# Two transformer layers on one core: the next block's preparation cut into single-engine steps, its stores on one queue, and a new timetable

## The chip, the cores and the metric

The kernel runs on one core of a Trainium2 chip. The metric is device time in microseconds (us) of the whole program, from the runs listed below. The engines are named as the profile names them: PE (TensorE, the matmuls), PEld (its weight loads), DVE (VectorE), ACT (ScalarE), POOL (GpSimd) and SP (SyncE, which here only issues DMA transfers). An engine carries out its instructions in program order. A letter q behind an engine's name (SPq, ACTq) marks an instruction that its sequencer issues, such as a DMA.

## The reference

Two layers, each an attention block and a gated block over 2048 tokens of width 448 (16 heads of 28, inner width 1792):

```python
x = A_x
for layer in range(2):
    # attention
    q, k, v = split_heads(layernorm(x) @ A_wqkv)
    x = x + merge_heads(softmax(q @ k.T * 28 ** -0.5) @ v) @ A_wo
    # gated
    n = layernorm(x)
    x = x + (sigmoid(n @ B_w_gate) * (n @ B_w_up)) @ B_w_down
```

Both layers use the same weights. All tensors are float32; the kernel computes the products from float16 high and low parts.

## The kernel before, in words

**Blocks and pairs.** In the gated part (`gated`, from L1342) the 2048 tokens are four blocks of 512, and the 1792 inner columns are seven pairs of 256. The work is done pair by pair: block 0 pairs 0 to 6, then block 1, and so on. For one pair `gate_and_up` (from L1503) multiplies the block's normalized tokens with the gate weights (m = 0) and the up weights (m = 1) by a seven-product scheme on half matrices. Its PE order is: `first(0)`, `first(1)`, `apart(0)`, `second(0)`, `second(1)`, `apart(1)`, `third(0)`, `third(1)`, `c11_c22(0)`, `c11_c22(1)`, `c21(0)`, `c21(1)`, `c12(0)`, `c12(1)`. After `first`, `second` and `third` ACT copies a PSUM bank called chain to the tiles one and two (L1509). After `c11_c22` DVE adds the bank side to one (L1525, called "the adds" below, one for each m); `c12` writes the same side bank, so PE cannot start `c12(0)` before the first add is done. Then ACT takes the sigmoid and DVE multiplies.

**Places.** Between these products there are six places, `along(0)` to `along(5)`, where other work is put: place 0 after `first(1)`, 1 after `second(1)`, 2 after `third(1)`, 3 after `c11_c22(1)`, 4 after the multiplications that follow `c21`, 5 at the pair's end. In place 0 and 1 go the splits of the pair before (`parts`, `rest`, L1393) and the addition of a finished part of the output to x. From block 1 on, PE also gets there the down products of the block before (`pieces`, bank dnp, L1436). Block 1 has four of these in a pair, since block 0's first three pairs use another path (`down`, L1484 to L1486); blocks 2 and 3 have seven.

**Preparation of the next block.** While block b is multiplied, block b + 1 is prepared by a list of steps, taken from a queue (`run_fill`); `portions(b, p)` says how many are taken in which place of which pair. For a block of the gated part the list was 16 steps: four of `norm` (row statistics, on DVE, with two small POOL operations each), four of `squares` (DVE scales a 128-token tile into xn, L288, and transposes it in 32 by 32 squares into xs, L305), one `store` and `gather` (four DMAs write xs to memory, L317; two read it back as xraw, transposed, L325 and L327), and seven of `half_steps`. These form differences t1 to t4 of quarters of xraw on DVE (`subtract`), and split seven operands into a float16 high part (ACT) and a low part (DVE: value minus high part) in xwide and xshort (`divide`); for the last three ACT copies half of the high part's tail (`double`, L389). The last block of layer 0 prepares the next layer's first two blocks with the same `store` and another ending; the last block of layer 1 prepares nothing.

**Slots and weights.** SBUF tiles of one size come from 19 slots in a first-in, first-out list of free ones (`Slots`): a tile that is given back goes to the end of the list, and the next tile to be made takes the one at its head. Whoever writes the new tile waits for the readers of the old one. xn, xs, xraw, xwide and xshort take slots of the same list as the weights. When a pair is done, its two weight slots are given back and the two weight loads (gu, m = 0 and m = 1) for the pair after the next are put on POOL's queue (`used_gu`, L1327), and from block 1 on one down weight (dn, L1339) behind them. POOL issues in order, so a load that waits for its slot holds those behind it.

Of the kernel before, what the change touches and what calls it, by code (L numbers as in the profile page):

```python
# [110 lines left out]
def interleaved_layers(ctx: ExitStack, tc: tile.TileContext, x_in, wqkv, wo, w_gate, w_up,  # L111
                       w_down, out):
    nc = tc.nc
# [7 lines left out]
    qrt = Slots(spool, "q", N_QUART)  # L121
# [133 lines left out]
    class Block:  # L255
# [86 lines left out]

        def steps(self):
            return self.squared() + [
                lambda: (self.store((nc.sync, nc.scalar)), self.gather())] + (
                        self.half_steps() if self.halves else
                        [lambda: self.ready(0, 1), lambda: self.ready(2, 3)])

# [4 lines left out]
        def half_steps(self):  # L353
            def cut(k, t):

                if self.turned:
                    return self.raw[:, k:k + 2, t * P:(t + 2) * P]
                return self.raw[:, k:k + 2, :].rearrange(
                    "p k (i t c) -> p k t i c", i=4, t=TB)[:, :, t:t + 2]

            def ordered(v):
                return v.rearrange("p k (t i c) -> p k t i c", t=2, i=4)

            def subtract(name, a, b):
                t = qrt.get(name, [P, 2, W // 2])
                if self.turned:
                    nc.vector.tensor_tensor(t, a, b, op=ALU.subtract)
                    return t
                a, b = [v if len(v.shape) == 5 else ordered(v) for v in (a, b)]
                for k in range(2):  # L370
                    nc.vector.tensor_tensor(ordered(t)[:, k], a[:, k], b[:, k],
                                            op=ALU.subtract)
                return t

            def divide(to, v):

                hi, lo = to[:, 0], to[:, 1]
                if len(v.shape) == 5:
                    for k in range(2):
                        nc.scalar.copy(ordered(hi)[:, k], v[:, k])  # L380
                        nc.vector.tensor_tensor(ordered(lo)[:, k], v[:, k], ordered(hi)[:, k],
                                                op=ALU.subtract)
                else:
                    nc.scalar.copy(hi, v)
                    nc.vector.tensor_tensor(lo, v, hi, op=ALU.subtract)

            def double(to):

                nc.scalar.copy(to[64:P, 0, 1], to[0:64, 0, 1])  # L389

            def r11():
                self.wide = big.get("xwide", [P, 4, 2, 2, W // 2], F16)
                self.short = big.get("xshort", [P, 3, 2, 2, W // 2], F16)
                self.t1 = subtract("t1", cut(0, 2), cut(0, 0))
                divide(self.wide[:, 0], cut(0, 0))

            def t1():
                self.t2 = subtract("t2", cut(2, 2), self.t1)
                divide(self.wide[:, 1], self.t1)
                qrt.put(self.t1)  # L400

            def t2():
                self.t3 = subtract("t3", cut(2, 2), cut(0, 2))
                divide(self.wide[:, 2], self.t2)

            def t3():
                self.t4 = subtract("t4", cut(2, 0), self.t2)
                nc.gpsimd.memset(self.t4[64:P, 1, :], 0.0)
                divide(self.wide[:, 3], self.t3)
                qrt.put(self.t2, self.t3)  # L410

            def r21():
                divide(self.short[:, 0], cut(2, 0))
                double(self.short[:, 0])

            def t4():
                divide(self.short[:, 1], self.t4)
                double(self.short[:, 1])
                qrt.put(self.t4)

            def r22():
                divide(self.short[:, 2], cut(2, 2))
                double(self.short[:, 2])
                big.put(self.raw)

            return [r11, t1, t2, t3, r21, t4, r22]

        def ready(self, *kts):
            if kts[0] == 0:
# [224 lines left out]
    def run_fill(fill, n=1):  # L654
        for _ in range(n):
            if fill:
                fill.popleft()()
# [610 lines left out]
    def out_project(outs, gate):  # L1268
        new_banks()
        nc.scalar.activation(warm, warm, AF.Sigmoid)  # L1270
        nc.scalar.reg_load(gate_scale, back.bitcast(I32)[0:1, 3:4])
        first = Block(0, True)
        steps = deque([first.turn_raw] + first.half_steps())
        early = 6

        def products(pm, t, kts):
            by_tokens(pm, outs.hi(t), outs.lo(t), outs.tail(t) if 3 in kts else None, gate.out,
                      kts)

        def add(pm, t):  # L1280
            nc.vector.scalar_tensor_tensor(x[:, t, :], pm, back[:, 1:2], x[:, t, :],
                                           op0=ALU.mult, op1=ALU.add)

        gate.load_gu()
        gate.load_usual()
        pms = [bank(t, "op")[:, 0:D] for t in range(early)]
        for t in range(early):
            products(pms[t], t, range(3))
        first.begin()
        for t in range(early):  # L1290
            products(pms[t], t, [3])
            add(pms[t], t)
            if t < TB:
                first.stats(t)
            if t >= TB:
                first.scale(t - TB)
        for j in range(early - TB, TB):
            first.scale(j)
        for t in range(early, NT):
            pm = bank(t if t < 8 else t % 4, "op")[:, 0:D]  # L1300
            products(pm, t, range(4))
            add(pm, t)
            if t >= 9:
                run_fill(steps, 2 if t == 9 else 1)
        big.put(*outs.kt, gate.out)
        run_fill(steps, 9)
        return first

# [42 lines left out]
    def gated(layer, first, wt, before_next):  # L1351
# [6 lines left out]
        steps = deque()  # L1358
# [135 lines left out]
        def gate_and_up(blk, w, at, operands):  # L1494
# [46 lines left out]
            def along(i):  # L1541
                for do in at[i]:
                    do()
# [27 lines left out]
            c12(1)  # L1571
            times(two[0][:, lo], two[1][:, lo])
            qrt.put(one[1], two[1])
            along(5)
            if made:
                made.late()
                return made
            hls = []
            for h in (one[0], two[0]):
# [95 lines left out]
    def portions(b, p):  # L1675

        if b == 0:
            steps = {0: {1: 4, 5: 1}, 1: {1: 4}, 2: {2: 1, 5: 2}, 3: {1: 1, 2: 2, 5: 1}}
        elif b < NB - 1:
            steps = {0: {1: 1, 2: 1}, 1: {1: 2, 2: 1}, 2: {1: 1, 2: 1}, 3: {1: 2},  # L1680
                     4: {2: 1, 5: 1}, 5: {1: 1, 2: 1}, 6: {1: 1, 2: 2}}
        else:
            steps = {0: {1: 2, 2: 1}, 1: {1: 2, 2: 1}, 2: {1: 1, 2: 2}, 3: {1: 2, 2: 2},
                     4: {1: 1, 2: 1}, 5: {1: 1, 2: 1}, 6: {1: 1, 2: 2, 5: 1}}
        return [steps.get(p, {}).get(i, 0) for i in range(6)]
# [88 lines left out]
```

## Time and profile before

| | |
|---|---|
| three runs | 1929.95 us median (1929.7 to 1930.24) |
| the profiled execution | 1928.17 us, its span 1926.5 us |
| PE busy | 1897.7 us, 99% of the span |
| DVE, ACT, POOL busy | 1413.9, 1365.6, 240.4 us |
| gated part, layer 0 | about 605 to 967 us of the span |
| gated part, layer 1 | about 1555 us to the end |

The times in the profile's rows count from the span's first instruction. A timeline row gives start, duration, engine, line, operation, the tiles written and read, their sizes and how many instructions were merged; in square brackets it gives how long the engine stood idle before it and what ended the wait. In a row of waits the numbers are the total, the count and the longest.

### The profile page before, as it was taken

How to read it: one execution, taken by the hardware profiler on the slowest of the kernel's cores; microseconds unless marked ns; L12 is line 12 of the kernel's file. 1: busy time of each engine (PE TensorE's matmuls, PEld its weight loads, DVE VectorE, ACT ScalarE, POOL GpSimd, SP SyncE). 2: the span in 40 equal slices, each digit the busy share in tenths (PEclk: the TensorE clock that was granted, in tenths of full speed). 3: DMA queues.
4: the chain of work that ended last, by engine and by line, in shares of the span. 5: the costliest groups of instructions: out<-in, count | busy, mean ns of one | idle time of the engine just before them, and what ended most of it. 6: DMA issues, size and time to landing. Idle time of an engine off the chain costs nothing. (4 is left out here: it accounts for less than half of the span.)

```text
span 1926.5 us, 56325 instructions
## 1 busy us (share of the span) xinstructions
PE 1897.7 (99%) x24317; PEld 1412.7 (73%) x24317; DVE 1413.9 (73%) x2816; ACT 1365.6 (71%) x1742; POOL 240.4 (12%) x467
## 2 busy tenths in 40 slices
PE   9999999999999999999999999999999999999999
PEld 4455655555556798999954578888888667989998
DVE  7648798688877597788664487778777767887764
ACT  5569999999983455454344799999999545554541
POOL 2013312232002021122100000000000011211110
PEclk9999999999999999999999999999999999999999
DMA  5565555354314556657634322112211235676752
GB/s 173 169 201 166 161 145 156 111 157 133 92 65 131 207 203 228 208 216 250 231 94 132 88 50 51 30 48 51 51 29 64 74 124 187 207 276 199 267 203 90
DMA packets 107298, 275.20 MB, mean 143 GB/s; under 512 B 12766, under 2 KB 63086, under 8 KB 106912
## 3 DMA queue, kind: packets, MB, share of 16 engines
q0 software_dynamic: 33088, 165.74, 24.4%
q1 hardware_dynamic: 67120, 102.33, 18.8%
q10 hardware_dynamic: 6832, 3.44, 0.8%
q8 instruction: 192, 3.15, 0.7%
q14 instruction: 66, 0.54, 0.1%
HBM read 213.39 MB, written 50.73 MB: 137 GB/s over the span
## 5 line engine op out<-in xcount | busy, mean ns | idle before, releaser
L1126 ACT ACTIVATE prob_s<-sc 128x1536 f32<-128x1536 f32 x659 | 892.3, 1484 | 6.6 <-PE sc L1111 3.3
L1162 PE MATMUL acc<-prob_s,val_s 128*32 128x256 f32 (+3 forms) x7754 | 595.9, 383 | 0.0
L1111 PE MATMUL sc<-qp_s 114*32 114x512 f16 x7896 | 581.2, 379 | 0.0
L527 PEld LDWEIGHTS <-gu_s 128*128 128x128 f16 x4368 | 427.1, 98 | 71.1 <-issue 23.8
L1111 PEld LDWEIGHTS <-qp_s 114*32 114x32 f16 x8192 | 311.3, 95 | 175.4 <-issue 77.3
L1162 PEld LDWEIGHTS acc<-prob_s,val_s 128*32 128x32 f32 x7754 | 326.2, 110 | 92.3 <-issue 7.3
L527 PE MATMUL chain<-xwide_s,gu_s 128*128 128x256 f16 x2016 | 248.3, 273 | 1.4 <-ACT two_q L1509 0.7
L1436 PE MATMUL dnp<-dn_s,hparts_s 128*128 128x224 f16 x2100 | 236.4, 260 | 0.0
L1436 PEld LDWEIGHTS <-hparts_s 128*128 128x128 f16 x2100 | 202.5, 98 | 5.1
L1509 ACT COPY one_q<-chain 128x256 f32<-128x256 f32 x224 | 81.2, 372 | 139.6 <-PE chain L527 118.0
L1142 DVE SCALAR_TENSOR_TENSOR power_q<-power_q,expo_q 128x512 f32<-128x512 f32 x222 | 153.7, 692 | 7.6
L527 PE MATMUL side<-xshort_s,gu_s 128*128 128x256 f16 x1120 | 141.2, 272 | 14.9 <-DVE one_q L1525 14.8
L512 PE MATMUL qkp<-xhl_s,wqk_s 128*128 128x512 f16 x616 | 138.0, 379 | 0.7 <-DVE xhl_s L491 0.3
L1525 DVE TENSOR_TENSOR one_q<-side,one_q 128x512 f32<-128x512 f32 x112 | 72.0, 685 | 65.0 <-PE side L527 50.5
L512 PEld LDWEIGHTS <-wqk_s 128*128 128x128 f16 x616 | 60.0, 98 | 70.1 <-ACT wqk_s L223 1.0
L1191 DVE STREAM_TRANSPOSE oturned_q<-acc 128x512 f32<-128x512 f32 x32 | 22.9, 716 | 118.4 <-PE acc L1162 118.4
L1327 POOL DMA_DIRECT2D gu_s<-gu_parts x104 | 56.0, 539 | 379.0 <-PE side L527 216.1
L1389 ACT CAST hparts_s<-hsums_q 128x256 f16<-128x256 f32 (+1 forms) x144 | 68.4, 489 | 33.5 <-DVE hsums_q L1401 20.4
L527 PE MATMUL side<-xwide_s,gu_s 128*128 128x256 f16 x672 | 91.7, 273 | 0.0
L1162 PE MATMUL acc<-power_q,val_s 128*32 128x256 f32 (+3 forms) x278 | 86.3, 393 | 0.0
L704 ACT ACTIVATE qkhl_q<-qkp 128x512 f16<-128x512 f32 x56 | 33.2, 593 | 74.0 <-PE qkp L512 70.6
L1536 ACT ACTIVATE one_q<-one_q 128x512 f32<-128x512 f32 x56 | 35.3, 630 | 68.7 <-DVE one_q L1525 68.7
(209 smaller groups left out, 2291.4 us busy)
## 6 DMA issues: line engine op xcount, KB each, us to landing
gu_s<-gu_parts POOLq DMA_DIRECT2D x104, 800.0 KB, 6.0
dn_s<-dn_parts POOLq DMA_DIRECT2D x50, 784.0 KB, 7.1
qp_s<-qk_scr SPq DMA_DIRECT2D x96, 224.0 KB
qk_scr<-qkhl_q SPq DMA_DIRECT2D x56, 256.0 KB
gu_parts<-pack_s POOLq DMA_DIRECT2D x14, 800.0 KB, 4.0
xraw_s<-xt_scr SPq DMA_DIRECT2D x12, 768.0 KB
xt_scr<-xs_s SPq DMA_DIRECT2D x34, 224.0 KB
qp_s<-qk_scr SPq DMA_DIRECT2D x64, 112.0 KB
```

Of the source, the lines that this page charges most:

```text
L512: nc.tensor.matmul(pm, w, x, start=(i == 0), stop=(i == len(terms) - 1))
L527: nc.tensor.matmul(pm, a, x, start=(first and i == 0), stop=(i == len(terms) - 1), skip_group_check=True)
L1111: nc.tensor.matmul(ps[32 * j:32 * j + 32, :], hd.k[:, keys], hd.q[:, qb * W:(qb + 1) * W], start=True, stop=True, tile_position=(0, 32 * j))
L1126: nc.scalar.activation(prob[:, 0:n, :], ps[:, 0:n, :], AF.Exp, scale=exp_scale)
L1142: nc.vector.scalar_tensor_tensor(p, p, c[k], y, op0=ALU.add, op1=ALU.mult)
L1162: nc.tensor.matmul(acc[qb * VC:(qb + 1) * VC, s], v[:, kc % TB, h, :], probs[c * NB + qb][:, s], start=(kc == 0 and a == 0), stop=(kc == N ...
L1327: queue.dma_start(self.gu[-1][m], gu_parts[p, m])
L1389: nc.scalar.copy(to[:, :, 0], a)
L1436: nc.tensor.matmul(pm, a[:, x, t], w[:, p, y], start=(begin and n == 0 and (j == 0 or alone)), stop=(n == 2), skip_group_check=True)
L1509: nc.scalar.copy(to, pm)
L1525: nc.vector.tensor_tensor(one[m], side[m], one[m], op=ALU.add)
L1536: nc.scalar.activation(out, v, AF.Sigmoid, scale=gate_scale)
```

## The change

It has five parts.

1. `divide` becomes `high` (ACT) and `low` (DVE). The high part of an operand is made in one step and its low part in the next one, so that within a step DVE uses nothing that ACT makes in it and ACT nothing that DVE makes in it. `double` is one step later still. The half steps become nine: the last low part and the last `double` are steps of their own (`last_low`, `last_rows`). All instructions are the same as before; only their order is new.
2. `store()` in `steps` is called without queues: all four DMAs go on SP's queue. Before, SP and ACT issued two each.
3. `made.late()` (two DVE subtractions of the pair itself) comes before `along(5)`, not after it.
4. In `portions` the 18 steps are laid out anew for block 0 and for blocks 1 and 2. The last block's row stays.
5. The steps after the attention's output product (`out_project`), which run the same half steps for block 0 itself, are taken 3, 2, 1, 1, ... at a time in place of 2, 1, 1, 1, ...

```diff
         def steps(self):
             return self.squared() + [
-                lambda: (self.store((nc.sync, nc.scalar)), self.gather())] + (
+                lambda: (self.store(), self.gather())] + (
...
             def r11():
...
                 self.t1 = subtract("t1", cut(0, 2), cut(0, 0))
-                divide(self.wide[:, 0], cut(0, 0))
+                high(self.wide[:, 0], cut(0, 0))
 
             def t1():
+                low(self.wide[:, 0], cut(0, 0))
                 self.t2 = subtract("t2", cut(2, 2), self.t1)
-                divide(self.wide[:, 1], self.t1)
+                high(self.wide[:, 1], self.t1)
+
+            def t2():
+                low(self.wide[:, 1], self.t1)
+                self.t3 = subtract("t3", cut(2, 2), cut(0, 2))
+                high(self.wide[:, 2], self.t2)
                 qrt.put(self.t1)
...
-            return [r11, t1, t2, t3, r21, t4, r22]
+            return [r11, t1, t2, t3, r21, t4, r22, last_low, last_rows]
...
             if t >= 9:
-                run_fill(steps, 2 if t == 9 else 1)
+                run_fill(steps, {9: 3, 10: 2}.get(t, 1))
...
             qrt.put(one[1], two[1])
+            if made:
+                made.late()
             along(5)
             if made:
-                made.late()
                 return made
...
         if b == 0:
-            steps = {0: {1: 4, 5: 1}, 1: {1: 4}, 2: {2: 1, 5: 2}, 3: {1: 1, 2: 2, 5: 1}}
+            steps = {0: {1: 4, 5: 5}, 2: {1: 1, 2: 1, 3: 1, 5: 1}, 3: {1: 1, 2: 1, 3: 1, 5: 1},
+                     4: {1: 1}}
         elif b < NB - 1:
-            steps = {0: {1: 1, 2: 1}, 1: {1: 2, 2: 1}, 2: {1: 1, 2: 1}, 3: {1: 2},
-                     4: {2: 1, 5: 1}, 5: {1: 1, 2: 1}, 6: {1: 1, 2: 2}}
+            steps = {0: {1: 2, 2: 1}, 1: {1: 2, 2: 1}, 2: {1: 1, 2: 2}, 3: {5: 1},
+                     4: {1: 1, 3: 1}, 5: {1: 1, 3: 1}, 6: {1: 1, 2: 1, 3: 1, 5: 1}}
```

In a row such as `2: {1: 1, 5: 1}` the first number is the pair, and inside the braces place and count follow.

More of the change, by code (lines that the diff above doesn't have):

```diff
@@ L373, in subtract, with high, low @@
                 return t
-            def divide(to, v):
+            def high(to, v):
+                hi = to[:, 0]
+                if len(v.shape) == 5:
+                    for k in range(2):
+                        nc.scalar.copy(ordered(hi)[:, k], v[:, k])
+                else:
+                    nc.scalar.copy(hi, v)
+            def low(to, v):
                 hi, lo = to[:, 0], to[:, 1]
@@ L379, in divide @@
                     for k in range(2):
-                        nc.scalar.copy(ordered(hi)[:, k], v[:, k])
                         nc.vector.tensor_tensor(ordered(lo)[:, k], v[:, k], ordered(hi)[:, k],
@@ L383, in divide @@
                 else:
-                    nc.scalar.copy(hi, v)
                     nc.vector.tensor_tensor(lo, v, hi, op=ALU.subtract)
@@ L394, in r11, with t4, r22, last_low @@
                 self.t1 = subtract("t1", cut(0, 2), cut(0, 0))
-                divide(self.wide[:, 0], cut(0, 0))
+                high(self.wide[:, 0], cut(0, 0))
             def t1():
+                low(self.wide[:, 0], cut(0, 0))
                 self.t2 = subtract("t2", cut(2, 2), self.t1)
-                divide(self.wide[:, 1], self.t1)
+                high(self.wide[:, 1], self.t1)
[3 more added lines that the diff above has]
+                high(self.wide[:, 2], self.t2)
                 qrt.put(self.t1)
-            def t2():
-                self.t3 = subtract("t3", cut(2, 2), cut(0, 2))
-                divide(self.wide[:, 2], self.t2)
             def t3():
+                low(self.wide[:, 2], self.t2)
                 self.t4 = subtract("t4", cut(2, 0), self.t2)
                 nc.gpsimd.memset(self.t4[64:P, 1, :], 0.0)
-                divide(self.wide[:, 3], self.t3)
-                qrt.put(self.t2, self.t3)
+                high(self.wide[:, 3], self.t3)
+                qrt.put(self.t2)
             def r21():
-                divide(self.short[:, 0], cut(2, 0))
+                low(self.wide[:, 3], self.t3)
+                high(self.short[:, 0], cut(2, 0))
+                qrt.put(self.t3)
+            def t4():
+                low(self.short[:, 0], cut(2, 0))
+                high(self.short[:, 1], self.t4)
+            def r22():
+                low(self.short[:, 1], self.t4)
                 double(self.short[:, 0])
-            def t4():
-                divide(self.short[:, 1], self.t4)
+                high(self.short[:, 2], cut(2, 2))
+                qrt.put(self.t4)
+            def last_low():
+                low(self.short[:, 2], cut(2, 2))
                 double(self.short[:, 1])
-                qrt.put(self.t4)
-            def r22():
-                divide(self.short[:, 2], cut(2, 2))
+                big.put(self.raw)
+            def last_rows():
                 double(self.short[:, 2])
-                big.put(self.raw)
-            return [r11, t1, t2, t3, r21, t4, r22]
+            return [r11, t1, t2, t3, r21, t4, r22, last_low, last_rows]
         def ready(self, *kts):
```

## The prediction

> **What bounds the kernel now.** I read the page's busy times first, then the waits of PE in one window for each block, then the timeline at each wait.
>
> ```profile
> span 1926.5 us, 56325 instructions
> PE 1897.7 (99%) x24317; PEld 1412.7 (73%) x24317; DVE 1413.9 (73%) x2816; ACT 1365.6 (71%) x1742; POOL 240.4 (12%) x467
> ```
>
> PE sets the end: its work is not changed, so only its idle time, 1926.5 - 1897.7 = 28.8 us, can be won. The waits of PE follow in this order: block 0 and block 1 of layer 0, then block 0 and block 1 of layer 1.
>
> ```profile
> PE side L527 <- DVE one_q L1525: 4.6, 2, 2.8
> PE chain L527 <- ACT one_q L1509: 1.7, 2, 1.4
> ...
> PE side L527 <- DVE one_q L1525: 2.4, 2, 1.8
> PE chain L527 <- ACT one_q L1509: 1.5, 1, 1.5
> PE chain L527 <- ACT two_q L1509: 0.7, 1, 0.7
> ...
> PE side L527 <- DVE one_q L1525: 4.5, 2, 2.7
> PE chain L527 <- ACT one_q L1509: 1.5, 1, 1.5
> ...
> PE side L527 <- DVE one_q L1525: 3.3, 2, 2.1
> ```
>
> That is 6.0 (of the 1.7, 0.2 is at the block's start and another matter), 4.6, 6.0 and 3.3 us: 19.9 in all. Blocks 2 and 3 have no PE wait of 0.1 us. So it is a question of four stretches, each with two or more waits, and of what is late next in each.
>
> **Block 0, where the stores come earlier.** Layer 0; pair 1 starts at 614.29, pair 2 at 629.17.
>
> ```profile
> 607.75 1.47 PE L527 MATMUL chain<-xwide_s,gu_s 128*128 128x256 f16 x12 [0.24 <-ACT one_q L1509]
> ...
> 615.42 0.51 DVE L288 TENSOR_SCALAR xn_s<-x,mv,rs 128x448 f32<-128x448 f32 x1
> ...
> 617.70 0.51 DVE L288 TENSOR_SCALAR xn_s<-x,mv,rs 128x448 f32<-128x448 f32 x1
> ...
> 620.39 0.65 DVE L305 STREAM_TRANSPOSE xs_s<-xn_s 128x448 f32<-128x448 f32 x1
> 621.07 0.85 SPq L317 DMA_DIRECT2D xt_scr<-xs_s  x2
> 621.33 0.54 POOL L1327 DMA_DIRECT2D gu_s<-gu_parts  x1 [6.04 <-DVE xs_s L305]
> 622.03 0.65 ACT L1509 COPY one_q<-chain 128x256 f32<-128x256 f32 x2 [3.67 <-DVE xs_s L305]
> 625.10 0.54 POOL L1327 DMA_DIRECT2D gu_s<-gu_parts  x1 [3.23 <-PE side L527]
> 632.73 0.39 SPq L325 DMA_DIRECT2D xraw_s<-xt_scr  x1
> 637.48 0.76 DVE L371 TENSOR_TENSOR t_q<-xraw_s 128x256 f32<-128x256 f32 x2 [10.01 <-DMA xraw_s<-xt_scr]
> 638.83 1.28 DVE L1525 TENSOR_TENSOR one_q<-side,one_q 128x512 f32<-128x512 f32 x2
> 639.57 1.30 PE L527 MATMUL side<-xshort_s,gu_s 128*128 128x256 f16 x10 [2.80 <-DVE one_q L1525]
> ```
>
> The reader is to see three waits. (a) ACT's two stores wait for DVE's transposes, and the copy behind them is 3.67 us late, PE 1.45. (b) DVE stands 10.01 us at the first difference, whose xraw is still on its way; the adds are behind it and PE loses 2.80. (c) In pair 3 DVE and ACT take turns within steps, and PE loses the other 1.8 of block 0's 4.6.
>
> (a) goes with the stores off ACT. All four squares now stand at the end of pair 0. Three took 620.39 + 0.65 - 617.70 = 3.3 us, so four from 615.42 end at about 619.9, against 621.04. The pair's own two low parts, which stood between the first square and the second, come after the fourth; DVE is done with all six at 621.1, as before. The first add (half of 1.28 us) then ends at 621.8. PE finishes `c11_c22` at 621.0, since its wait (a) began there, and `c21` 1.1 us later (10 matmuls), so it needs the add at 622.1. So nothing takes the place of (a).
>
> (b) is a chain: stores 621.07 to 632.73 (11.7 us), gather to DVE's first use 4.75 us, from there to PE 2.1 us. Its last link grows: the next step, which now stands between the first one and the adds, adds a second subtraction of 0.7 us, so 2.8. The middle one stays. The first is the open price: four stores on one queue. The rows for it:
>
> ```profile
> 723.50 2.87 SPq L317 DMA_DIRECT2D xt_scr<-xs_s  x2
> 723.77 0.53 POOL L1327 DMA_DIRECT2D gu_s<-gu_parts  x1 [4.66 <-DVE xs_s L305]
> 733.32 0.38 SPq L325 DMA_DIRECT2D xraw_s<-xt_scr  x1
> 733.80 0.53 POOL L1327 DMA_DIRECT2D gu_s<-gu_parts  x1 [9.50 <-DMA xt_scr<-xs_s]
> ...
> 936.66 2.99 SPq L317 DMA_DIRECT2D xt_scr<-xs_s  x4
> 942.85 0.38 SPq L325 DMA_DIRECT2D xraw_s<-xt_scr  x1
> ```
>
> SP alone with no weight load beside it took 6.2 us (936.66 to 942.85). Two queues with one weight load beside them took 9.8 (723.50 to 733.32), with two loads 11.7 (621.07 to 632.73, loads at 621.33 and 625.10). In the changed block 0 one load falls into the stores, the one that takes xn's slot and is let go by the same transposes; the next one takes xs's slot and waits for the stores. I take 9.8, nearest in what lies beside it, and keep 6.2 and 11.7 as ends; SP's four issues end after 3.0 us, two queues' after 2.9, so issue is no difference. The Trainium skill (DMA: Bandwidth & Descriptors, Issuing engines are not separate DMA queues) says that transfers from any engine run on the same 16 DMA engines and that more issuers save only issue time; by it the one queue also takes 9.8.
>
> So the gather goes at 619.9 + 9.8 = 629.7, DVE starts at 634.5 and PE goes on at 637.3. Without (a), PE would be there at 636.77 - 1.45 = 635.3: a wait of 2.0 us stays, of 2.8. The first high part, now in place 1, holds ACT's copies until 635.7, inside the same wait. (c): in pair 3 every step has its inputs from the step before; DVE has 1.45 us of it ahead of the adds and PE's time for `third` hides that, so 1.8 goes. Block 0 then keeps 2.1 of 6.0 us in each layer. The two steps more after the output product remove the 0.24 us of the first row, also in each layer.
>
> **Block 1, where a weight load becomes late.** Pairs start at 696.68, 707.50 and 718.31, so an unhindered one takes 10.8 us.
>
> ```profile
> 701.07 0.62 DVE L279 BATCH_NORM_STATS2 st<-x 128x6 f32<-128x448 f32 x1
> ...
> 701.82 0.59 DVE L279 BATCH_NORM_STATS2 st<-x 128x6 f32<-128x448 f32 x1
> ...
> 703.75 1.25 DVE L1525 TENSOR_TENSOR one_q<-side,one_q 128x512 f32<-128x512 f32 x2
> 705.26 1.25 PE L527 MATMUL side<-xshort_s,gu_s 128*128 128x256 f16 x10
> ...
> 707.50 1.47 PE L527 MATMUL chain<-xwide_s,gu_s 128*128 128x256 f16 x12
> 713.53 0.65 DVE L305 STREAM_TRANSPOSE xs_s<-xn_s 128x448 f32<-128x448 f32 x1
> 718.31 1.47 PE L527 MATMUL chain<-xwide_s,gu_s 128*128 128x256 f16 x12
> ...
> gu_s<-gu_parts POOLq DMA_DIRECT2D x1, 800.0 KB, 6.8
> ...
> gu_s<-gu_parts POOLq DMA_DIRECT2D x1, 800.0 KB, 8.2
> ```
>
> All that PE lost here (4.6 and 3.3) had causes that the new layout takes away: the stores on ACT (1.45), the first difference too soon after its gather (0.58 and 2.08), steps with turns (the rest). Now gather and first difference are some 16 us apart, in pair 2's place 2 and pair 3's place 5, and the gather needs 14.6. But two things come.
>
> First, DVE has one more step in pairs 0 and 1: 0.8 us more of norm by pair 0 (701.07 to 701.82 is one), then a norm and two squares (3.1 us) against two norms and a square (2.7). In pair 1 the adds move from 703.75 to 705.0; the first ends 0.7 later, at 705.7, and PE wants it at 705.26. I charge 0.5 us in layer 0, 0.35 in layer 1.
>
> Second, slots. Following the list of free slots by hand: before, xn and xs came free in pair 3, and the two weight loads put on POOL at its end took them, for pair 5. Now they come free in pair 2, and the loads at its end take them, for pair 4. The m = 1 load waits for the stores: it is issued 10.3 us after their start (723.50 to 733.80) and lands 6.8 us later, in layer 1 8.2 (the last two rows, which are these two loads), so 17.1 to 18.5 after xs is ready. xs was ready 6.7 us into pair 2 (713.53 + 0.65 - 707.50); with DVE's delay 7.4. So it lands 24.5 to 25.9 us after pair 2's start; `first(1)` of pair 4 wants it after 2 x 10.8 + 0.65 (`first(0)`, half of the 12 matmuls at 707.50) = 22.3. PE waits 2.2 to 3.6 us; I take 3.0 in each layer. Behind this load POOL holds a down weight and the next pair's loads, which have a pair's time. In blocks 2 and 3 a pair takes 12.5 us and the same sum gives 1 to 2 us to spare.
>
> **The sum.** 12.0 + 7.9 - 2 x 2.1 - (0.5 + 3.0) - (0.35 + 3.0) + 0.5 = 9.3 us less. The profiled execution took 1928.17, so 1918.9; the runs' median is 1.8 above it: 1920.7, rounded to 1921. One thing more can move it:
>
> ```profile
> 637.66:641.07 3.41, 1.50 (x12) 1.16 (x12) 3.25 (x8) 1.55 (x4) 0.50 (x1) 1.00 0.00 0
> ...
> 1688.97:1692.38 3.41, 1.37 (x13) 1.20 (x13) 3.25 (x8) 1.61 (x4) 0.37 (x1) 1.00 1.01 372
> 1692.38:1695.79 3.41, 3.41 (x20) 2.55 (x18) 3.01 (x10) 2.17 (x5) 1.21 (x3) 0.50 0.85 281
> ```
>
> These are time windows (PE busy first, the granted clock third from last). After 1688.97:1692.38, with PE busy 1.37 of 3.41 us, the clock was 0.50 for the next 3.41 us, which costs 1.7; after the first row, with 1.50 busy, it was not. Layer 1's 2.7 us wait was followed by such a window too. So waits over about 2 us can cost 1.7 more. Two did before; block 1's new waits would make about as many, so I count no change, and 1.7 either way. The Trainium skill (TensorE: Matmul & The Clock Gate, Part 1) asks for a whole idle window of about 3.4 us before half clock; by that rule no wait here costs extra, and the row with PE busy 1.37 us disagrees.
>
> **Rivals.** (1) *The one queue is quicker beside a load.* At 6.6 us block 0's first difference comes 3 us earlier and block 1's load in time: waits of 0.9 us are left of 19.9, and the two slow windows go: 19.5 + 3.4 less, about 1907. For it: 936.66. Against: that row has no load beside it. (2) *The waits only move.* Each us of store time counts once in every one of the four stretches. At 11.7 us, as in block 0 before, 9.3 shrinks to 1.7: 1928. For it: two queues took that long once. Against: two loads did that. (3) *Slower: the single queue loses its turns to the weight load.* From 12.1 us on there is no gain; at 13.4 the stretches lose 14.4 us, and block 2 and 3's loads come 1 to 2 us late as well (some 5 in all): 1928.2 + 1.8 + 10 = 1940. For it: beside one load even two queues lost 9.8 - 6.2 = 3.6 us. Against: SP's own issue pace is no slower. The skill's rule of turns between queue rows (the same page, Queues, rings and completion order) would give one row half of the turns instead of two thirds; no run here shows it. (4) *The new order does not part the engines*: DVE, whose adds at 703.75 have no idle time before them, pays back in one place what it wins in another: 1930.
>
> **Chances.** Forecast 0.50, with its own range 1917 to 1926 (store time 9.2 to 10.6 is -2.4 to +3.2, the load's landing 1.5, a window 1.7); rival 1 0.17; rival 2 0.18; rival 3 0.08; rival 4 0.07. A change of 0.2% (3.9 us) is about what a measurement of this kernel tells from none. Below 1926 lie the forecast, less 0.02, and rival 1: 0.65. Rivals 2, most of 4 and the rest of the forecast are within: 0.26. Rival 3 is slower: 0.09. The range goes from 1907 to 1930: rival 3 and the far sides of 1 and 4 are left out.
>
> **What would show it.** Right: no ACT wait at L305; SP's four stores in block 0 from about 619.7, the gather 9.8 us later; a PE wait near 637 of some 2 us; a PE wait of 2 to 4 us at the start of block 1's pair 4 ended by the landing of gu, in both layers. Wrong: a gather 6 to 7 us or 12 us and more after the first store; no wait for gu in block 1; waits of PE for DVE's adds in block 1's pairs 4 to 6 or block 0's pair 1.

## The result, and the profile after

The changed kernel took 1915.56 us (median of 4 runs, 1912.09 to 1918.24), the kernel before 1929.83 us (median of 4, 1929.58 to 1930.24) beside it. The ratio is 0.9925, with a 95% interval of 0.9908 to 0.9942: 14 us less. The profiled execution was the slowest of the four, 1918.24 us. Below the change, line numbers are 18 higher than before: the matmuls are L545 (L527 before), ACT's copies L1527 (L1509), the adds L1543 (L1525), the weight loads L1345 (L1327). L279 to L371 stay.

The page first, then the waits of PE in the same four stretches as in the prediction: block 0 and block 1 of layer 0, then of layer 1. The numbers of a wait are the total, the count and the longest.

```profile
span 1916.4 us, 56353 instructions
PE 1897.9 (99%) x24317; PEld 1405.8 (73%) x24317; DVE 1412.8 (74%) x2816; ACT 1366.0 (71%) x1742; POOL 240.6 (13%) x467
...
PE chain L545 <- ACT one_q L1527: 2.5, 1, 2.5
PE side L545 <- DVE one_q L1543: 0.8, 1, 0.8
...
PE chain L545 <- DMA gu_s<-gu_parts: 2.0, 1, 2.0
...
PE side L545 <- DVE one_q L1543: 2.0, 1, 2.0
PE chain L545 <- ACT one_q L1527: 1.1, 1, 1.1
...
PE chain L545 <- DMA gu_s<-gu_parts: 2.1, 1, 2.1
```

PE's busy time is what it was, and the span is 10.1 us shorter. The stretches lose 3.3, 2.0, 3.1 and 2.1 us: 10.5, where they lost 19.9. Block 1 shows no wait for ACT or for the preparation any more, but one for a weight load, which none of the four stretches had before.

The timeline of block 0's pair 1 and 2 shows the chain behind the first pair of waits. A row is start, duration, engine, line, operation, tiles, sizes, and in brackets the idle time before it and what ended that.

```profile
619.85 2.33 SPq L317 DMA_DIRECT2D xt_scr<-xs_s  x4
620.12 0.55 POOL L1345 DMA_DIRECT2D gu_s<-gu_parts  x1 [7.59 <-DVE xs_s L305]
629.43 0.39 SPq L325 DMA_DIRECT2D xraw_s<-xt_scr  x1
629.82 1.07 POOL L1345 DMA_DIRECT2D gu_s<-gu_parts  x2 [9.16 <-DMA xt_scr<-xs_s]
635.49 0.76 DVE L371 TENSOR_TENSOR t_q<-xraw_s 128x256 f32<-128x256 f32 x2 [9.55 <-DMA xraw_s<-xt_scr]
636.59 1.25 PE L545 MATMUL chain<-xshort_s,gu_s 128*128 128x256 f16 x10 [2.55 <-ACT one_q L1527]
637.56 0.42 DVE L371 TENSOR_TENSOR t_q<-xraw_s,t_q 128x256 f32<-128x256 f32 x1 [0.30 <-DMA xraw_s<-xt_scr]
638.64 2.29 PE L545 MATMUL side<-xshort_s,gu_s 128*128 128x256 f16 x10 [0.79 <-DVE one_q L1543]
...
1573.84 0.39 SPq L325 DMA_DIRECT2D xraw_s<-xt_scr  x1
1578.52 0.76 DVE L371 TENSOR_TENSOR t_q<-xraw_s 128x256 f32<-128x256 f32 x2 [8.15 <-DMA xraw_s<-xt_scr]
1581.67 0.42 DVE L371 TENSOR_TENSOR t_q<-xraw_s,t_q 128x256 f32<-128x256 f32 x1 [1.39 <-DMA xraw_s<-xt_scr]
1582.75 1.56 PE L545 MATMUL side<-xshort_s,gu_s 128*128 128x256 f16 x10 [1.95 <-DVE one_q L1543]
```

The stores go 1.2 us earlier, take 9.6 us (619.85 to 629.43) instead of 11.7, and DVE has the gathered rows 2.0 us earlier (635.49, against 637.48). But PE is no longer held up in pair 1, so it comes to pair 2's end sooner too. And its wait comes in two pieces. The first (2.55 us here) is for ACT's copies: the first high part, which reads xraw, stands ahead of them on ACT and starts when the gather lands. The second (0.79 us; 1.95 in layer 1) is for DVE's adds, behind the second subtraction, whose second instruction stands idle once more (0.30 and 1.39 us) for the second of the gather's two transfers.

In block 1 the stores and the load that waits for them:

```profile
713.70 2.31 SPq L317 DMA_DIRECT2D xt_scr<-xs_s  x4
723.27 0.38 SPq L325 DMA_DIRECT2D xraw_s<-xt_scr  x1
723.70 0.53 POOL L1345 DMA_DIRECT2D gu_s<-gu_parts  x1 [9.20 <-DMA xt_scr<-xs_s]
...
730.78 0.83 PE L545 MATMUL chain<-xwide_s,gu_s 128*128 128x256 f16 x6 [1.98 <-DMA gu_s<-gu_parts]
```

The load put at 723.70, once the stores had been read out of xs, is the one that PE waits for at 730.78.

### The profile page after: what moved, and what is told of

Same layout as the page of the kernel before. It is cut to its first block, busy times and chain, and to the rows that moved or that the text cites. A ratio compares the mean times of both kernels' runs of the same rounds, so it can differ in the third digit from the quotient of the medians.

```text
span 1916.4 us, 56353 instructions
## 1 busy us (share of the span) xinstructions
PE 1897.9 (99%) x24317; PEld 1405.8 (73%) x24317; DVE 1412.8 (74%) x2816; ACT 1366.0 (71%) x1742; POOL 240.6 (13%) x467
## 3 DMA queue, kind: packets, MB, share of 16 engines
q8 instruction: 192, 3.15, 0.7%
## 5 line engine op out<-in xcount | busy, mean ns | idle before, releaser
L545 PEld LDWEIGHTS <-gu_s 128*128 128x128 f16 x4368 | 428.0, 98 | 60.3 <-issue 8.1
L1180 PEld LDWEIGHTS acc<-prob_s,val_s 128*32 128x32 f32 x7754 | 317.9, 110 | 100.8 <-issue 7.6
L545 PE MATMUL chain<-xwide_s,gu_s 128*128 128x256 f16 x2016 | 249.0, 273 | 4.1 <-DMA gu_s<-gu_parts 4.0
L1527 ACT COPY one_q<-chain 128x256 f32<-128x256 f32 x224 | 82.0, 372 | 132.0 <-PE chain L545 131.3
L545 PE MATMUL side<-xshort_s,gu_s 128*128 128x256 f16 x1120 | 142.1, 274 | 3.0 <-DVE one_q L1543 2.7
L1543 DVE TENSOR_TENSOR one_q<-side,one_q 128x512 f32<-128x512 f32 x112 | 72.0, 684 | 83.4 <-PE side L545 83.4
L1345 POOL DMA_DIRECT2D gu_s<-gu_parts x104 | 56.0, 540 | 365.7 <-PE side L545 183.3
L545 PE MATMUL side<-xwide_s,gu_s 128*128 128x256 f16 x672 | 92.3, 274 | 0.0
L1407 ACT CAST hparts_s<-hsums_q 128x256 f16<-128x256 f32 (+1 forms) x144 | 68.4, 489 | 33.1 <-DVE hsums_q L1419 20.6
```

The costliest lines, as they stand in the source:

```text
L545: nc.tensor.matmul(pm, a, x, start=(first and i == 0), stop=(i == len(terms) - 1), skip_group_check=True)
L1180: nc.tensor.matmul(acc[qb * VC:(qb + 1) * VC, s], v[:, kc % TB, h, :], probs[c * NB + qb][:, s], start=(kc == 0 and a == 0), stop=(kc == N ...
L1345: queue.dma_start(self.gu[-1][m], gu_parts[p, m])
L1407: nc.scalar.copy(to[:, :, 0], a)
L1527: nc.scalar.copy(to, pm)
L1543: nc.vector.tensor_tensor(one[m], side[m], one[m], op=ALU.add)
```

## The experiments

A table of all of them but one comes first. "Waits" is the sum of PE's waits from 600 us on, from the view of waits of each profile, without one of 0.2 us in the attention part that all have; "half" counts the stretches of 3.41 us between 600 us and 1910 us in which the granted clock was 0.5 (half of 3.41 us is 1.7 us; why they come is a matter of its own, below). Ratios are against runs of the kernel before on the same chip.

| kernel | profiled us | waits | half | median us | ratio (95%) |
|---|---|---|---|---|---|
| before | 1928.17 | 20.3 | 2 | 1929.83 | 1 |
| after | 1918.24 | 10.3 | 3 | 1915.56 | 0.9925 (0.9908 to 0.9942) |
| after again | 1916.22 | 9.6 | 2 | 1915.07 | 0.9925 (0.9911 to 0.9938) |
| before, stores on SP | 1927.19 | 20.6 | 2 | 1929.03 | 1.0001 (0.9992 to 1.001) |
| before, steps divided | 1916.93 | 12.2 | 1 | 1916.93 | 0.9937 (0.9924 to 0.9951) |
| both of these | 1916.59 | 10.3 | 2 | 1916.97 | 0.9938 (0.9925 to 0.9952) |
| after, two queues | 1923.88 | 16.0 | 4 | 1923.88 | 0.9963 (0.9949 to 0.9977) |
| after, buffer edit | 1902.2 | 0.2 | 0 | 1902.6 | 0.9855 (0.984 to 0.987) |
| after, block 0 later | 1908.65 | 5.6 | 0 | 1910.56 | 0.9897 (0.9882 to 0.9912) |
| after, waits filled | 1913.07 | 5.3 | 0 | 1913.07 | 0.9919 (0.9905 to 0.9932) |
| before, buffer edit | 1915.98 | 11.0 | 0 | 1915.79 | 0.9933 (0.9919 to 0.9946) |
| before, buffer edit and SP | 1918.17 | 12.2 | 2 | 1919.48 | 0.9948 (0.9934 to 0.9962) |

With 1.7 us for each half stretch, the waits account for the differences of the profiled times from before to within 3.5 us, for most to within 1 to 2 (with the waits filled, the added matmuls count as well). That rest was not traced.

### The stores alone

```diff
-                lambda: (self.store((nc.sync, nc.scalar)), self.gather())] + (
+                lambda: (self.store(), self.gather())] + (
```

> The kernel before with one edit: its stores are issued by SyncE alone. My theory: ScalarE no longer stands behind its two stores, so the wait of 1.45 us at the second pair of block 0 goes in both layers, and that of block 1 in the first layer. But the end of the chain store, gather, first difference is set by the transfers: the store runs beside a weight load and takes 9 to 12 us by one queue as by two, so in block 0 the next wait of the same pair (2.80 and 2.69 us) stays or grows by what was won, and the waits on turn-taking (1.78, 1.79, 0.73, 1.26 us) stay. Total of the TensorE gaps 20 to 23.3 us against 23.28 before; time 1927.0 to 1930. Rival, that each wait is worth itself: 4.35 us less, 1925.5. Rival, that one queue is the gain (the store shorter by 3 us or more): 1920 or less.

No difference (1.0001), and the gaps say why. The timeline at block 0's pair 1 and 2, in layer 0:

```profile
620.87 2.34 SPq L317 DMA_DIRECT2D xt_scr<-xs_s  x4
621.14 0.54 POOL L1327 DMA_DIRECT2D gu_s<-gu_parts  x1 [6.04 <-DVE xs_s L305]
623.29 0.54 POOL L1327 DMA_DIRECT2D gu_s<-gu_parts  x1 [1.61 <-PE side L527]
632.28 0.39 SPq L325 DMA_DIRECT2D xraw_s<-xt_scr  x1
639.39 0.97 PE L527 MATMUL side<-xshort_s,gu_s 128*128 128x256 f16 x6 [4.44 <-DVE one_q L1525]
```

The wait on ACT (1.45 us) is gone and the next one is 4.44 us where it was 2.80. The store took 11.4 us on one queue, 11.7 on two, beside two weight loads each time. So the theory holds: this wait is worth nothing as long as the gather sets the end of the pair.

### The divided steps alone, and with the stores

The first kernel takes `high` and `low` in place of `divide`, with the timetable of before and the two added steps at its end; the second has the stores on SP as well. Both keep the change's part 5, which is worth 0.24 us of PE's waits in each layer.

```diff
-            steps = {0: {1: 4, 5: 1}, 1: {1: 4}, 2: {2: 1, 5: 2}, 3: {1: 1, 2: 2, 5: 1}}
+            steps = {0: {1: 4, 5: 1}, 1: {1: 4}, 2: {2: 1, 5: 2}, 3: {1: 1, 2: 2, 5: 2},
+                     4: {1: 1}}
...
-                     4: {2: 1, 5: 1}, 5: {1: 1, 2: 1}, 6: {1: 1, 2: 2}}
+                     4: {2: 1, 5: 1}, 5: {1: 1, 2: 1}, 6: {1: 1, 2: 2, 3: 1, 5: 1}}
```

> The kernel before with the steps divided as in the kernel after, and the timetable of before with the two added steps put at the end; the stores stay on two queues. My theory: the waits on turn-taking (1.78, 1.79, 0.73, 1.26 us and smaller ones, 7.3 us in sum) go, those behind the stores (1.45 us three times) and on the first difference (2.80, 2.69, 0.58, 2.08 us) stay: 1922.5, range 1920.5 to 1925. Rival, that dividing the steps only moves the wait into the next step: 1928 or more, with gaps of ScalarE on VectorE as long as before. Rival, that the timetable is what gains: no change, 1929.8.

> The divided steps and the stores on SyncE alone, with the timetable of before (the two added steps at its end). It differs from the kernel after in the timetable and in where the last half of the preparation is called. My theory: the two edits are worth nearly all of it; in block 0 waits of 3 to 4 us each layer are left, in block 1 up to 2.5 us: 1915.6 to 1918.5, at most 3 us above the kernel after. Rival, that the timetable is the main source of the gain: 1921 or more. Rival, that the effects of the two edits add up to less than each alone: above the faster of the two runs with one edit.

Divided steps alone give 12 us (0.9937), more than was expected. The waits of the first kernel and then of the second:

```profile
PE side L545 <- DVE one_q L1543: 6.3, 4, 2.5
PE chain L545 <- ACT one_q L1527: 4.3, 3, 1.5
PE chain L545 <- ACT two_q L1527: 1.6, 2, 0.8
```

```profile
PE side L545 <- DVE one_q L1543: 8.7, 4, 3.3
PE chain L545 <- ACT two_q L1527: 1.6, 2, 0.8
```

The waits fell from 20.3 to 12.2 us, near the 7.3 us of turn-taking that were expected to go, with the 0.5 of part 5; the three waits of 1.45 us behind ACT's stores are still there. With the stores on SP these go and 2.4 of their 4.3 us come back as longer waits for DVE, so the sum is 10.3. Yet the time is the same (1916.97 against 1916.93): waits of 1.45 and 2.2 us that were apart have become one of 3.3, and the half stretches are two instead of one. Against the kernel after, which differs from the second kernel by the timetable and the place of `made.late()`, 0.9938 and 0.9925 can't be told apart. So dividing the steps, with part 5, brings nearly all of the 14 us.

### The kernel after again

No edit.

> The kernel after, unchanged, to see which of its times vary from execution to execution: its runs so far lie 6 us apart, those of the kernel before 0.7 us. My theory: the waits that set the rest depend on transfers that share the DMA engines, and each wait of over 2 us can bring a stretch of 3.4 us at half clock, worth 1.7 us; so the profile shows the same places with waits that differ by up to 1 us and zero to three such stretches, and the median lies between 1912 and 1918.3. Rival, that the spread was of one chip: all times within 1 us of one another.

The spread is there in a second set of runs too (1912.12 to 1916.43), and goes with the clock: the five runs had a mean granted clock of 0.997 to 0.999, the fastest 0.999 and the two slowest 0.997. The kernel before spreads as much in this series (15 runs, 1926.9 to 1932.0), so the 0.7 us between its first four runs does not set the two kernels apart. The waits are where they were; their sum is 0.7 us less.

### After, with the stores on two queues

```diff
-                lambda: (self.store(), self.gather())] + (
+                lambda: (self.store((nc.sync, nc.scalar)), self.gather())] + (
```

> The kernel after with one edit taken back: its stores are issued by SyncE and ScalarE again. My theory: ScalarE stands behind its two stores, TensorE waits for it for 0.8 to 1.5 us in the pair of the store, and what is lost there is missing from the later wait on the first difference, so the sum of the gaps grows by 0 to 2.5 us, while the two shorter waits bring in fewer stretches at half clock than one of 3 us: 1914 to 1917, no difference that can be told. Rival, that the store from one queue is what the new timetable needs: 1919 or more.

My theory was wrong here: 1923.88, and by the ratios (0.9963 against 0.9925) 7 us slower than the kernel after. Block 0 in layer 0:

```profile
619.57 0.92 ACTq L317 DMA_DIRECT2D xt_scr<-xs_s  x2
621.99 2.72 PE L545 MATMUL chain<-xwide_s,gu_s 128*128 128x256 f16 x12 [5.87 <-ACT one_q L1527]
```

The new timetable puts the stores at the end of pair 0, so ACT's two wait for the transposes ahead of all of pair 1's copies, and PE stops for 5.87 us in each layer. I had taken the wait from the old place, in pair 1, where it was 1.45. So the edit to the queue is worth nothing with the old timetable and 7 us with the new one: it is what lets the four squares stand at the end of pair 0.

### After, with the buffers handed on in another order

xn's slot goes to the head of the list of free ones, so that xraw takes it, and the weight loads take slots that have long been free. The clearing of 64 rows of xraw moves to the first half step.

```diff
-            big.put(xn)
+            if self.halves:
+                big.free.appendleft(big.held.pop(id(xn))[0])
+            else:
+                big.put(xn)
...
             def r11():
+                if not self.turned:
+                    nc.gpsimd.memset(self.raw[64:P, 3, :], 0.0)
```

> The kernel after, with the buffer of the normalised rows handed to the gathered rows instead of to the next load of gate weights (and the clearing of 64 rows of the gathered tile moved behind that). The loads then wait for nothing of the preparation and are through before the store. My theory: the store took 9.1 to 10.1 us because a load was started in the same moment; alone it takes the 6.2 us of the one store that ran alone. The gather lands 3.4 us or more earlier, the waits of block 0 (3.3 and 3.0 us) and those on gate weights in block 1 (2.0 and 2.1 us) all go, with them up to three stretches at half clock of 1.7 us: 1899 to 1906. Rival, that the store is slow for another reason (one queue, rows of 512 bytes, the reading of the columns): the store stays over 9 us, only the waits on gate weights go, 1909 to 1912. Rival, that the loads then collide elsewhere or buffers come free too late: 1915 or more.

1902.6 us (1902.2 to 1903.26), 13 us less than the kernel after, 28 less than before. The waits, and block 0:

```profile
PE chain L548 <- DMA gu_s<-gu_parts: 0.2, 1, 0.2
...
611.22 1.29 POOL L1348 DMA_DIRECT2D gu_s<-gu_parts  x2 [0.28 <-PE chain L548]
619.67 3.01 SPq L320 DMA_DIRECT2D xt_scr<-xs_s  x4
625.92 0.39 SPq L328 DMA_DIRECT2D xraw_s<-xt_scr  x1
630.56 0.76 DVE L372 TENSOR_TENSOR t_q<-xraw_s 128x256 f32<-128x256 f32 x2 [4.80 <-DMA xraw_s<-xt_scr]
```

The loads are issued 8 us ahead of the stores, these take 6.25 us, and DVE has the rows 4.9 us earlier than in the kernel after. From 600 us on, two waits of 0.2 us are all that the view still shows for PE, and the mean granted clock is 1.0 in each of the four runs, which lie 1.1 us apart. So the store's 9.6 us are the price of the one load that xn's release starts in the same moment (0.27 us after the stores in block 0), not of the one queue and not of the rows' form. The same profile holds a comparison: the store at 874.63, for the next layer's first block, which the edit does not reach, still has a load issued 0.27 us into it and takes 10.16 us.

### After, with the first difference later

```diff
-            steps = {0: {1: 4, 5: 5}, 2: {1: 1, 2: 1, 3: 1, 5: 1}, 3: {1: 1, 2: 1, 3: 1, 5: 1},
-                     4: {1: 1}}
+            steps = {0: {1: 4, 5: 5}, 2: {5: 1}, 3: {1: 1, 2: 1, 3: 1, 5: 1},
+                     4: {1: 1, 2: 1, 3: 1, 5: 1}}
```

> The kernel after with block 0's four steps of pair 2 put one pair later: the first difference after the gather is taken at the end of pair 2, and pairs 3 and 4 take four steps each. My theory: the two waits of pair 2 (3.3 us in the first layer, 3.0 in the second) come from steps that stand ahead of the gather's landing; put behind it they go whole, with the stretch of half clock that follows each of them (1.7 us), and the waits on gate weights in block 1 stay (2.0 and 2.1 us): 1905 to 1909. Rival, that the wait only moves to pair 4 or to the start of block 1, since the steps are then too many for the pairs left: 1913 to 1917. Rival, that the stretches at half clock do not depend on the waits: 1908.5 to 1909.5.

The mechanism as expected, but 1910.56 us (0.9897) where 1905 to 1909 were expected, and a part of the rival: some of the wait moved on. Block 0's pair 2 has no wait left; instead there are two of 0.43 and 0.46 us in each layer where its pair 4 passes into pair 5, with four steps in that pair beside its own splits (the second row; the other sum is 0.9 too), and block 1's waits for the loads stay:

```profile
PE chain L545 <- DMA gu_s<-gu_parts: 3.8, 2, 2.0
PE chain L545 <- ACT one_q L1527: 0.9, 2, 0.5
```

The four runs fall in two: 1907.97 and 1908.65 with a clock of 0.999 and 1.0, 1912.46 and 1912.73 with 0.998. The profile is of a run with the clock at 1.0. That the two slower runs have half stretches at block 1's waits of 2.0 us is likely from their clock, but neither was profiled.

### Matmuls in the waits

To see whether half clock follows idle time, the first of two kernels puts matmuls that nobody reads into the waits of the kernel after, into the free half of bank chain. They restart the sum of their whole bank, so that a part of pair 2's products in block 0 (m = 1) and of pair 4's in block 1 (m = 0) is lost.

```diff
+            def idle_work(m, k, n):
+                for _ in range(n):
+                    of_halves(chain[m][:, hi], w[0], blk, k, True)
...
+            if fill == "raw":
+                idle_work(1, 1, 2)
             c21(0)
```

> The kernel after with matmuls that nobody reads, into a half bank that is not used, put into TensorE's waits: three groups of six (2.3 us) in block 0's pair 2, and two groups (1.5 us) ahead of the late weight load in block 1's pair 4, in each layer. The preparation, the transfers and the real matmuls stay as they are. My theory: the stretches of 3.4 us at half clock follow idle time of TensorE. The idle time in these places falls by 2.3 and 1.5 us and is made up by the added matmuls, and the stretches there (three in the profile of the kernel after, at 638, 1584 and 1676 us) go: 1910 to 1913.5. Rival, that the clock drops for another reason: 1914.5 to 1917, stretches as before. Rival, that the added matmuls cost their own time (7.6 us): 1920 or more.

1919.91 us (ratio 0.9943, 0.993 to 0.9957), and nothing learned in block 0: the added matmuls themselves waited for ACT's copies out of that bank (gaps of 2.48 and 1.23 us ahead of them), so they filled no wait and cost their time behind it. In block 1, where they could run, its profile shows no half stretch.

The second kernel writes to 64 columns of another bank, whose other columns hold block 0's output, without restarting the sum.

```diff
+            def unread(n):
+                for i in range(n):
+                    nc.tensor.matmul(spare[0], w[0][:, i % 14], blk.wide[:, 1, 0, 0, 0:512 - D],
+                                     start=False, stop=True, skip_group_check=True)
...
+            if fill == "raw":
+                unread(20)
             c21(0)
```

> As the run before it with matmuls put into the waits, but so that these depend on nothing that is late: in block 0's pair 2 they write 64 columns of another bank that nobody reads (20 ahead of the first wait, 8 ahead of the second), in block 1's pair 4 they add to a half bank that nobody reads. My theory: the stretches at half clock follow idle time of TensorE. The gaps in these places fall from 3.3, 3.0, 2.0 and 2.1 us to 1.5 us or less each, no late instruction comes earlier, and the mean granted clock rises from 0.998 to 0.9995 or more: 2 to 4 us less than the kernel after, 1911 to 1913.5. Rival, that the clock drops for another reason: clock 0.998 and 1914.5 to 1917. Rival, that the added matmuls take longer than the waits: 1917 or more with a clock of 0.9995 or more.

As expected in time, though only just: 1913.07 us (0.9919), 1 us below the kernel after by the ratios, within both intervals. Block 0's waits fell less than expected, to 2.4 and 2.1 us a layer instead of 1.5; block 1's to 0.5. The clock tells more: 0.999 or 1.0 in all five runs, where the nine runs of the kernel after had 0.997 to 0.999. That is what was to be told apart; what it is worth in time is within the noise. The windows at block 0's wait, here and then in the kernel after (PE's busy time is first, the granted clock third from last):

```profile
635.47:638.88 3.41, 1.49 (x18) 1.27 (x18) 2.66 (x7) 2.20 (x6) 0.00 (x0) 1.00 0.87 310
638.88:642.30 3.42, 3.23 (x22) 2.05 (x22) 3.42 (x9) 1.19 (x4) 0.00 (x0) 1.00 0.02 7
```

```profile
634.75:638.17 3.42, 1.25 (x10) 0.97 (x10) 2.38 (x7) 1.93 (x6) 0.00 (x0) 1.00 0.92 334
638.17:641.58 3.41, 2.94 (x13) 1.83 (x13) 3.41 (x8) 1.35 (x3) 0.00 (x0) 0.50 0.02 9
```

### Before, with the buffer edit, without and with the stores on SP

The edit to xn's slot alone, put into the kernel before; the second kernel has the stores on SP beside it.

> The kernel before with the buffer edit alone: the normalised rows' buffer goes to the gathered rows, so that the loads of gate weights do not start with the store. My theory: the four waits on the first difference (2.80, 2.69, 0.58, 2.08 us) go since the store is 3 us shorter, with them the two stretches at half clock (1.7 us each); ScalarE still stands behind its stores (1.45 us three times) and the waits on turn-taking stay (7.3 us): gaps 8 us less, 1917 to 1921. Rival, that the collision only mattered after the change: 1927 or more. Rival, that the later stages are late too and the waits move on to them: 1922 to 1927.

> The same buffer edit together with the stores on SyncE alone, the steps undivided. My theory: with undisturbed stores the first difference is no longer what ends last, so that ScalarE's wait behind its stores is worth itself: 4 us less than with the buffer edit alone, 1913 to 1917, where the same queue edit gave nothing in the kernel before. Rival, that the stores' queue is worth nothing in the old timetable, whatever the store takes: the same as the buffer edit alone, 1917 to 1921.

The buffer edit alone gives 13 us (0.9933), as much as the whole change, with no step divided. The stores on SP make it slower by 3.7 us, where I expected 4 us less; the intervals overlap a little (0.9919 to 0.9946 and 0.9934 to 0.9962). Block 0 of the two kernels:

```profile
621.75 1.25 SPq L320 DMA_DIRECT2D xt_scr<-xs_s  x2
623.49 1.25 PE L530 MATMUL chain<-xshort_s,gu_s 128*128 128x256 f16 x10 [1.79 <-ACT one_q L1512]
626.13 0.54 POOL L1330 DMA_DIRECT2D gu_s<-gu_parts  x1 [3.76 <-PE side L530]
628.00 0.39 SPq L328 DMA_DIRECT2D xraw_s<-xt_scr  x1
634.75 0.76 DVE L372 TENSOR_TENSOR t_q<-xraw_s 128x256 f32<-128x256 f32 x2 [6.25 <-DMA xraw_s<-xt_scr]
```

```profile
621.02 2.98 SPq L320 DMA_DIRECT2D xt_scr<-xs_s  x4
623.44 0.54 POOL L1330 DMA_DIRECT2D gu_s<-gu_parts  x1 [1.81 <-PE side L530]
630.21 0.39 SPq L328 DMA_DIRECT2D xraw_s<-xt_scr  x1
635.26 0.76 DVE L372 TENSOR_TENSOR t_q<-xraw_s 128x256 f32<-128x256 f32 x2 [9.35 <-DMA xraw_s<-xt_scr]
```

The next load is let go by PE, at the end of the pair. Where ACT is stuck, PE is late, the load goes out 4.4 us into the store, and the store still takes 6.25 us. Where ACT is free, PE is 1.8 us ahead and the load goes out 2.4 us into the store, which takes 9.2. The wait that the queue edit removes had kept the load off the store. But it did not keep it off the gather: from there to DVE's first use it took 6.75 us in the first kernel and 5.05 in the second, so the rows came only 0.5 us apart, and the store explains little of the 3.7 us. PE's waits from 600 us on differ by 1.2 us (11.0 and 12.2): ACT's wait is gone, and one on the first difference stands in its place (2.24 and 2.08 us). The second profile has a half stretch behind each of these two and the first has none, which is 3.4 us. (The profiles lie only 2.2 us apart, since PE lost 1.7 us more before 600 us in the first.) What follows for the theory: the store's time is set by the load that starts in its first microseconds, in every one of these kernels, and the gather behind it can pay for a load that starts later.

## Why the prediction was right, and where it was not

**The result** lies in its range and on its side, 5 us below the time it gave. On its own scale, the profiled execution, it said 1918.9, and 1918.24 was measured. The rest is the step from the profile to the median: it added 1.8 us, since the profile of before was below its median; the profiled execution of after was 2.7 us above its own. The kernel after spreads over 6 us, and the prediction had nothing on that.

**The sum of the waits** was right: it left 11.1 us of 19.9, and 10.5 were left. That it came so close is in part luck, since its terms were off both ways: what was left to block 0 was 2.2 us too small over the two layers, what was left to block 1 some 2.5 us too large. And the profile's 1918.24 holds a third half stretch (1.7 us) that was not counted, made up for by about as much that was not traced. The first premise, that only PE's idle time can be won, was too narrow: matmuls slowed by half clock count as busy, and where the half stretches went, busy time fell too (1892.1 us with the buffer edit, 1897.7 before).

*The store* was priced at 9.8 us beside one load. Measured: 9.6 in block 0 of both layers and 9.5 to 9.6 in block 1. The choice between the ends 6.2 and 11.7, by what lies beside the row, held; the buffer edit showed that 6.2 is the time without a load, one queue or two.

*Block 0's wait* was mis-sized: 2.0 us said (2.1 in the sum), 3.3 and 3.1 measured. Two terms failed. From gather to DVE it took 4.75 us, which layer 1 kept (4.68), but layer 0 did not (6.06); what made these transfers slower in layer 0 was not settled (the two loads issued behind the gather are there in both layers, and in the kernel with the buffer edit, with 4.64; it is no accident of one run, since the second profile of the kernel after has 5.98 and 4.62). And the last link was "a second subtraction of 0.7 us, so 2.8": it took 3.15 and 4.23 us, since that subtraction also reads what the gather's second transfer brings and stands idle for it (the 0.30 and 1.39 us above). A step that was moved up in front of the adds brought its own wait with it, which the prediction did not look for.

*Block 1's late load* came as said, at pair 4's `first(1)`, in both layers, but was mis-sized the other way: 2.0 and 2.1 us, said 3.0 (2.2 to 3.6). The load was put 10.0 us after the stores, not 10.3, and landed 7.0 us later (in layer 1, 9.9 and 7.2): near the lower of the two rows, 6.8 and 8.2. *The later adds in pair 1* were charged 0.5 and 0.35 us and cost 0.14 each.

*The wait (a) behind ACT's stores* went and nothing took its place, as said. But its worth was read from the old place. Alone the edit is worth nothing, since the gather's wait takes all of it up; under the new timetable it is worth 7 us. *The turn-taking (c)* went whole, as said, and the run with the divided steps alone shows that this is where most of the gain is from: its waits fell by 8.1 us, against 10.0 with the whole change.

*The slow clock* was counted as unchanged, two stretches: three were in the profile. Over the runs it was near it: a mean clock of 0.998 in 15 runs of before and also in the 9 runs of after.

**The rivals.** One queue that is quicker beside a load (1): no, beside a load it took 9.1 to 10.1 us in all blocks. Its size of gain was to be had, but by taking the load away. Waits that only move (2): true of the store edit taken alone, not of the change. The queue that loses its turns (3): no; beside two loads one queue took 11.1 to 11.4 us, two took 11.6 to 11.8. The order that does not part the engines (4): no.

## What to carry to other kernels

Ask of each transfer on the path what starts in its first microseconds, and which release starts it: here the tile that the store's own producer gave back let a weight load go, and handing that slot to another tile was worth as much as all the rescheduling, and 13 us more on top of it. Price an edit in the order in which it will run: a wait on an in-order engine costs by what is queued behind it, and the same queue edit was worth nothing, 7 us, or a loss of 3 to 4 us, depending on the timetable and the buffers beside it. When a step is moved ahead of others, look up which part of a gather it reads.

## What the runs showed of the hardware

**The store and a load beside it.** In the gated part of all these kernels the same four transfers, from the first issue to the issue of the gather, took 6.2 to 7.3 us where no weight load was issued in their first 2.5 us (6.8 or more only where an earlier load was still landing), 8.8 to 10.3 us where one was issued 0.3 or 2.4 us into them, and 11.1 to 11.8 us where two were. Where a single load was issued 4.0 and 4.4 us into them (the kernel before with the buffer edit), they took 6.4 and 6.2 us, but the gather behind them took 7.4 and 6.8 us to DVE's first use, where the kernel before has 4.5 to 5.0, with or without its stores on SP. Beside a load, SP alone was 0.4 us quicker than SP and ACT in the mean of 21 pairs of stores (from 0.4 slower to 1.1 quicker), and no different without one. The Trainium skill (DMA: Bandwidth & Descriptors, Issuing engines are not separate DMA queues) says that more issuers bring no bandwidth; these runs agree.

**Half clock.** The granted clock changes at the ends of windows of 3.41 us. In the traces of all these kernels, from 600 to 1910 us, 17 windows at full clock had PE busy for 1.47 us or less, and all 17 were followed by a window at half clock; of those with 1.6 us or more none was. In between lie 1.49 and 1.50 us, each followed by full clock, and one of 1.51 by half. PE's busy time bears out the 1.7 us of a half stretch roughly: 1892.1 to 1893.0 us in the three profiles without one and without added matmuls, 1895.9 to 1897.7 in the five with two. Four windows from the second profile of the kernel after show the two sides, at the same wait for a load in layer 0 and 1:

```profile
728.12:731.54 3.42, 1.46 (x15) 1.14 (x14) 3.08 (x9) 1.72 (x5) 0.96 (x2) 1.00 1.04 380
731.54:734.95 3.41, 3.41 (x17) 2.35 (x18) 1.36 (x4) 1.19 (x3) 0.00 (x0) 0.50 1.02 416
1673.60:1677.01 3.41, 2.00 (x19) 1.80 (x20) 1.98 (x5) 1.13 (x3) 0.00 (x0) 1.00 1.03 399
1677.01:1680.43 3.42, 3.42 (x35) 3.12 (x33) 2.75 (x7) 2.32 (x7) 0.00 (x0) 1.00 1.01 416
```

The waits were of 1.96 and 1.95 us; one fell into one window, the other over the end of one. So a wait of about 2 us costs 1.7 us more or nothing by where it falls. That the spread of the kernel after comes from this is likely and not shown: the kernel without waits has a spread of 1.1 us, but two runs of the kernel after with clocks of 0.999 and 0.997 took the same time (1915.54 and 1915.58). The Trainium skill (TensorE: Matmul & The Clock Gate, Part 1) has half clock follow a whole idle window; the rows agree on the window's length and differ on the rest: 1.46 of 3.42 us were busy, and only two of the 17 windows had PE idle throughout (in the kernel after with two queues).
